# A second queue for the first loads and another bank for the parameters, in the opening of a one-core layer kernel

## The chip, the cores and the metric

One core of one Trainium2 chip. The metric is the device time of one execution in microseconds (us), told as the median of several executions. A profiled execution also leaves a trace, whose span is some 2.2 us shorter than the device time; statements about single waits come from traces, statements about what is faster from the times. In the traces PE is TensorE (matmuls), PEld its weight loads, DVE VectorE, ACT ScalarE, POOL GpSimd, and SPq and ACTq are the queues on which SyncE and ScalarE issue transfers.

## The reference

```python
x  = A_x                                  # (1, 2048, 448), bf16
xn = layernorm(x)                         # over the last axis, 448 wide
s  = state_space(xn, ...)                 # complex recurrence over 2048 steps, plus xn * Dskip
g  = silu((silu(xn @ w_gate) * (xn @ w_up)) @ w_down)    # 448 -> 1792 -> 448
return x + s * g
```

For the change only the very beginning matters: the first 128-row tiles of `x` are normalised and transposed, and multiplied with the first 512 columns of `w_gate` and `w_up`.

## The kernel before

The work is cut into four blocks of 512 rows (four tiles of 128). The opening treats the first block in two halves: tiles 0 and 1 (the left half, banks called `one`) while tiles 2 and 3 are still being normalised, then tiles 2 and 3 (the right half, banks called `gp` and `up`). Warm-up matmuls on constants keep TensorE busy until data is there.

```python
warm(12, D)                       # 12 pairs of 448-column matmuls on constants
load_x1(0)                        # tile 0, SyncE's queue
load_x(1, 3)                      # tiles 1 and 2 in one transfer, SyncE's queue
nc.scalar.activation(of_table[:], half_pi[:], ACT.Sqrt)      # makes ScalarE load its table
load_w(Wg, B_w_gate, 0, 512)
load_x1(3)
for c0, h in ((0, H2), (256, H1)):                           # up weights in two halves of columns
    load_w(Wu, B_w_up, c0, c0 + 256, part=0)
    nc.sync.dma_start(out=Wu[h, KF, 0:512], in_=B_w_up[blk(KF), 0:512][h])
# ... further weights and tiles ...
```

`rb` holds the right half's four banks, two pairs of one for gate and one for up. Before they hold sums they take the transposes of tile 2 (pair 0) and tile 3 (pair 1), and the turned parameters:

```python
def turn_tile(n, half):
    tps = [halves_of(b[:, half[0] : half[1]].bitcast(BF16))[:, 0] for b in rb[n - 2]]
    turned(n, tps)                                           # eight transposes on TensorE
    nc.vector.tensor_copy(out=xT_of(n)[:, :, H1], in_=tps[0])
    ...                                                      # H2: VectorE for tile 2, ScalarE for tile 3

def third():                      # runs between the left half's matmuls
    turn_tile(2, left)

def fourth():                     # likewise, eight matmuls later
    tv = params_turned(rb[0][0][:, right[0] : right[1]])     # two matmuls into pair 0's gate bank
    turn_tile(3, right)
    nc.vector.tensor_copy(out=pcol[:], in_=tv)
    power(dtv[:], euler[:], pcol[:, 0:KT, 0])

def right_half():                 # tile 2 for both pairs, then tile 3 for both pairs
    for f0, c, kw in ((0, left, dict(steps=tiles)), (2, right, dict(late=True))):
        gu_matmuls(0, ...)
```

In the left half the up matmuls come as six that need the first half of the up weights' columns, six that need the second half, tile 2's transposes, eight, the parameters and tile 3's transposes, eight.

## Time and profile before

| before | us |
|---|---|
| device time, median of 3 | 183.27 |
| device time in the rounds with the changed kernel, median of 6 | 183.12 (182.75 to 183.39) |
| span of the profiled execution | 180.9 |

To read the opening, cut it at five events of TensorE: the first transposes, tile 2's transposes, the right half's first matmul and the first full-width (512-column) matmul. This is the table of stretches of the kernel before (columns: stretch, length, then busy time and number of instructions of PE, PEld, DVE, ACT and POOL, granted clock, share of the DMA engines, GB/s).

```profile
0.00:5.59 5.59, 3.79 (x24) 1.74 (x24) 2.91 (x21) 2.56 (x6) 3.73 (x14) 1.00 0.67 192
5.59:8.70 3.11, 3.00 (x78) 2.56 (x80) 2.37 (x10) 2.61 (x7) 0.00 (x0) 1.00 0.93 251
8.70:10.15 1.45, 1.42 (x38) 1.07 (x33) 1.16 (x5) 1.07 (x4) 0.00 (x0) 1.00 1.08 369
10.15:13.30 3.15, 3.15 (x72) 2.81 (x73) 1.72 (x5) 1.33 (x5) 0.45 (x1) 1.00 1.07 358
13.30:180.90 167.60, 164.22 (x1303) 79.51 (x1297) 156.81 (x233) 115.36 (x239) 10.28 (x10) 1.00 0.22 55
```

Only the lengths matter here. The busy column does not show what is lost: a matmul's modelled end lies 0.1 us and more behind the point at which the next can start, so a TensorE that waits 0.2 us still reads as busy. The last stretch, 93% of the span, is the part that no one touches.

### The profile page before, as it was taken

How to read it: one execution, taken by the hardware profiler on the slowest of the kernel's cores; microseconds unless marked ns; L12 is line 12 of the kernel's file. 1: busy time of each engine (PE TensorE's matmuls, PEld its weight loads, DVE VectorE, ACT ScalarE, POOL GpSimd, SP SyncE). 2: the span in 40 equal slices, each digit the busy share in tenths (PEclk: the TensorE clock that was granted, in tenths of full speed). 3: DMA queues.
4: the chain of work that ended last, by engine and by line, in shares of the span. 5: the costliest groups of instructions: out<-in, count | busy, mean ns of one | idle time of the engine just before them, and what ended most of it. 6: DMA issues, size and time to landing. Idle time of an engine off the chain costs nothing.

```text
span 180.9 us, 3868 instructions
## 1 busy us (share of the span) xinstructions
PE 175.6 (97%) x1507; PEld 87.7 (48%) x1507; DVE 165.0 (91%) x271; ACT 122.9 (68%) x258; POOL 14.5 (8%) x24
## 2 busy tenths in 40 slices
PE   8799999999999999999999999999999999999992
PEld 3684444544444555555454444455454444455551
DVE  4869799999999989989999999999999999999962
ACT  4758779997789999298689675943268778601110
POOL 7012400000000000700000001400000000000001
PEclk9999999999999999999999999999999999999999
DMA  5998564899000000035000000052000000001111
GB/s 154 284 363 233 107 121 87 150 252 372 16 0 4 2 0 4 0 71 149 2 4 0 0 4 0 3 113 80 27 0 4 0 0 4 0 0 51 51 62 43
DMA packets 25330, 12.72 MB, mean 70 GB/s; under 512 B 14944, under 2 KB 25312, under 8 KB 25312
## 3 DMA queue, kind: packets, MB, share of 16 engines
q1 hardware_dynamic: 25040, 12.41, 25.7%
q8 instruction: 12, 0.20, 0.4%
q10 hardware_dynamic: 144, 0.07, 0.1%
q14 instruction: 6, 0.05, 0.1%
q0 software_dynamic: 128, 0.00, 0.0%
HBM read 7.23 MB, written 1.84 MB: 50 GB/s over the span
## 4 chain that ended last, share of the span: by engine, by line
PE 95%; DMA 2%; DVE 1%; SPq 0%; issue 0%
PE gp L477 26%; PE hd L620 23%; PE up L477 20%; PE y L658 12%; PE pb L477 12%; PE one L477 2%; DMA x_all<-in_A_x_dram 2%; DVE xn L281 0%; DVE stats_of L269 0%; DVE ob L684 0%; SPq L138 0%; DVE t L680 0%; PE tp L333 0%; PE gp L333 0%; PE y L664 0%
## 5 line engine op out<-in xcount | busy, mean ns | idle before, releaser
L477 PE MATMUL gp<-xT,Wg 64*128 64x512 bf16 (+2 forms) x400 | 82.4, 364 | 0.0
L477 PE MATMUL up<-xT,Wu 64*128 64x512 bf16 (+2 forms) x400 | 82.3, 364 | 0.0
L477 PEld LDWEIGHTS <-Wg 64*128 64x128 bf16 x444 | 38.4, 94 | 24.1
L477 PEld LDWEIGHTS <-Wu 64*128 64x128 bf16 x428 | 38.1, 94 | 19.0 <-issue 0.2
L620 PE MATMUL hd<-Wd,Vt 128*128 128x448 bf16 x224 | 43.5, 352 | 0.0
L607 ACT ACTIVATE gs<-gp 128x512 bf16<-128x512 f32 x52 | 31.4, 605 | 14.0 <-PE gp L477 13.9
L620 PEld LDWEIGHTS <-Vt 128*128 128x128 bf16 x224 | 21.8, 98 | 20.5 <-issue 0.2
L608 ACT ACTIVATE us<-up 128x512 bf16<-128x512 f32 x52 | 31.7, 609 | 0.0
L625 ACT ACTIVATE sg<-hd 128x448 bf16<-128x448 f32 x16 | 8.6, 536 | 25.0 <-PE hd L620 24.3
L477 PE MATMUL pb<-xT,BT 64*128 64x512 bf16 (+1 forms) x224 | 21.9, 349 | 0.0
L612 DVE TENSOR_TENSOR Vt<-gs,us 128x2048 bf16<-128x2048 bf16 (+1 forms) x16 | 17.1, 1075 | 0.3 <-ACT us L608 0.3
L477 PEld LDWEIGHTS <-BT 64*128 64x128 bf16 x224 | 10.7, 94 | 11.4 <-issue 0.7
L551 DVE TENSOR_TENSOR_SCAN bu_re<-rcol,H_re,ere 128x512 bf16<-128x512 f32 x12 | 15.1, 1269 | 0.1
L658 PE MATMUL y<-C,H_re 128*128 128x448 bf16 (+2 forms) x68 | 15.1, 342 | 0.0
L512 ACT ACTIVATE bu_re<-pb 128x512 bf16<-128x512 f32 (+1 forms) x20 | 10.0, 530 | 4.8 <-PE pb L477 4.8
L658 PE MATMUL y<-C,H_im 128*128 128x448 bf16 (+2 forms) x51 | 11.9, 342 | 0.0
L551 DVE TENSOR_TENSOR_SCAN bu_im<-rcol,H_im,eim 128x512 bf16<-128x512 f32 x9 | 11.4, 1263 | 0.0
L317 ACT ACTIVATE xn<-x_all,off_of,rstd 128x384 bf16<-128x384 bf16 (+1 forms) x16 | 8.1, 587 | 3.6 <-POOL off_of L311 3.6
L522 ACT ACTIVATE bu_im<-bu_re 64x512 bf16<-64x512 bf16 x16 | 10.0, 628 | 0.3
L680 DVE TENSOR_TENSOR t<-t,sg 128x448 f32<-128x448 f32 x15 | 9.4, 625 | 0.9
L684 DVE TENSOR_TENSOR sg<-t,x_all 128x448 bf16<-128x448 f32 x15 | 9.4, 625 | 0.5
L545 DVE TENSOR_TENSOR tmp<-bu_im,ST 128x2048 bf16<-128x2048 bf16 x8 | 9.7, 1218 | 0.0
(122 smaller groups left out, 183.8 us busy)
## 6 DMA issues: line engine op xcount, KB each, us to landing
out_dram<-sg SPq DMA_DIRECT2D x15, 112.0 KB, 1.7
Wd<-in_B_w_down_dram SPq DMA_DIRECT2D x1, 1568.0 KB, 10.1
Wg<-in_B_w_gate_dram SPq DMA_DIRECT2D x3, 384.0 KB, 5.1
x_all<-in_A_x_dram SPq DMA_DIRECT2D x1, 896.0 KB, 5.6
Wu<-in_B_w_up_dram SPq DMA_DIRECT2D x4, 192.0 KB, 4.5
Wu<-in_B_w_up_dram SPq DMA_DIRECT2D x2, 384.0 KB, 5.5
x_all<-in_A_x_dram SPq DMA_DIRECT2D x3, 224.0 KB, 5.4
Wg<-in_B_w_gate_dram SPq DMA_DIRECT2D x3, 128.0 KB, 4.9
```

The source lines that it names most:

```text
L477: mm = nc.tensor.matmul(out[:, a:b], lhsT=w[h, d, :], rhs=xT[h, d, q * W + c0 + a : q * W + c0 + b], start=(first and m == 0 and cut is cu ...
L512: nc.scalar.activation(to, pair[i][0], ACT.Copy)
L522: nc.scalar.activation(out[a], in_[b], ACT.Copy)
L545: nc.vector.tensor_tensor(out=of(out, n), in0=of(a, n), in1=of(b, n), op=op)
L551: nc.vector.tensor_tensor_scan(out=T["b"][c][:, k, :], data0=rcol[:, k : k + 1].to_broadcast([P, W]), data1=T["e"][c][:, k, :], initial=in ...
L607: nc.scalar.activation(gs[:, i + j, :], gp_[:], ACT.Silu)
L608: nc.scalar.activation(us[:, i + j, :], up_[:], ACT.Copy)
L612: nc.vector.tensor_tensor(out=Vt[:, f0 : f0 + n, :], in0=gs[:, 0:n, :], in1=us[:, 0:n, :], op=ALU.mult)
L620: nc.tensor.matmul(hd, lhsT=Vt_of[q][:, fi, j * P : (j + 1) * P], rhs=Wd[:, fi, :], start=(fi == 0), stop=(fi == NF - 1),)
L658: nc.tensor.matmul(y[:, c0:c1], lhsT=h, rhs=C2[:, n, c0:c1], start=(n == 0), stop=(n == NS - 1))
L680: nc.vector.tensor_tensor(out=t[:], in0=y, in1=sg[:, c0:c1], op=ALU.mult)
L684: adds.tensor_tensor(out=ob, in0=t[:], in1=x_all[:, m, c0:c1], op=ALU.add)
```

## The change

The intent: tiles 1 and 2 are issued by ScalarE at once instead of by SyncE as its second transfer; the weights behind them move up; the parameters go to tile 3's bank, so that the right half's first pair is free of them, and the right half goes pair by pair, so that tile 3's bank is wanted later; one warm-up pair less makes room for the earlier tiles.

```diff
-    def load_x(n0, n1):
-        nc.sync.dma_start(
+    def load_x(n0, n1, eng=nc.sync):
+        eng.dma_start(
@@
-    warm(12, D)
+    warm(11, D)
     load_x1(0)
-    load_x(1, 3)
+    load_x(1, 3, nc.scalar)
@@ in sums(..., by_tile=True)
+            order = [(n, two, cut) for cut in cuts for n, two in enumerate(pairs)]
+            if not by_tile:
+                order.sort(key=lambda o: o[0])
@@ in fourth()
-        tv = params_turned(rb[0][0][:, right[0] : right[1]])
+        tv = params_turned(rb[1][0][:, left[0] : left[1]])
@@ in right_half()
-        for f0, c, kw in ((0, left, dict(steps=tiles)), (2, right, dict(late=True))):
+        for f0, c, kw in ((0, left, dict(steps=tiles, by_tile=False)), (2, right, dict(late=True))):
```

More of the change, by code (lines that the diff above doesn't have):

```diff
@@ L461, in told_of, with sums @@
         tc.add_manual_dep(mm.ins, notice, SYNC, reason="other half")
-    def sums(q, pairs, eng=nc.gpsimd, turn=False, late=False, behind={}, steps=None):
+    def sums(q, pairs, eng=nc.gpsimd, turn=False, late=False, behind={}, steps=None, by_tile=True):
         left = []
@@ L470, in sums @@
             cuts = steps if steps and first else [None]
-            for n, two, cut in [(n, two, cut) for cut in cuts for n, two in enumerate(pairs)]:
+            order = [(n, two, cut) for cut in cuts for n, two in enumerate(pairs)]
+            if not by_tile:
+                order.sort(key=lambda o: o[0])
+            for n, two, cut in order:
                 for m in range(4 - share):
```

## The prediction

> **What bounds the kernel now.** I read the page first: its busy row and its chain that ended last.
>
> ```profile
> PE 175.6 (97%) x1507; PEld 87.7 (48%) x1507; DVE 165.0 (91%) x271; ACT 122.9 (68%) x258; POOL 14.5 (8%) x24
> PEclk9999999999999999999999999999999999999999
> ...
> PE 95%; DMA 2%; DVE 1%; SPq 0%; issue 0%
> ```
>
> The reader is to see one engine, PE (the TensorE), busy nearly throughout at a full granted clock, and 95% of the chain on it. No line of the matmuls gets shorter by this change, so it can only take away time in which TensorE stands still. Next, therefore, the chain in order of time for the first 16 us (columns: start us, length us, what): everything that is not a matmul lies there, and in the last 4 us, which the change doesn't touch.
>
> ```profile
> 1.18 3.01 DMA x_all<-in_A_x_dram
> 4.19 0.02 issue
> 4.21 0.64 DVE stats_of L269
> ...
> 5.65 0.41 DVE xn L281
> 6.05 0.05 issue
> 6.10 0.29 PE tp L333 x8
> 6.39 0.06 PE warm L191 x2
> 6.45 2.42 PE one L477 x56
> ...
> 9.68 0.44 PE one L477 x8
> 10.12 0.03 issue
> 10.15 0.21 PE gp L477
> ```
>
> The chain begins with the transfer of tiles 1 and 2 (issued at 1.18, landed at 4.19), goes through tile 1's statistics, normalised tile and transposes, and is on TensorE from 6.10. The third view is the timeline, which shows the two places concerned: the start, and the change-over from the left to the right half near 10 us (start, length, engine, line, operation, idle before).
>
> ```profile
> 0.72 1.28 ACT L198 ACT_TABLE_LOAD   x1 [0.72 <-PEq L909]
> 0.72 0.40 SPq L138 DMA_DIRECT2D x_all<-in_A_x_dram  x1
> ...
> 1.18 0.42 SPq L141 DMA_DIRECT2D x_all<-in_A_x_dram  x1
> ...
> 2.85 0.63 DVE L269 BATCH_NORM_STATS2 stats_of<-x_all 128x6 f32<-128x448 bf16 x1 [1.04 <-DMA x_all<-in_A_x_dram]
> ...
> 3.33 0.77 PEld L191 LDWEIGHTS <-const-bfloat16-1.0 64*128 64x128 bf16 x8 [0.20 <-issue]
> ...
> 3.51 0.20 DVE L270 BATCH_NORM_AGGREGATE mv<-stats_of 128x2 f32<-128x9 f32 x1
> ...
> 4.21 0.63 DVE L269 BATCH_NORM_STATS2 stats_of<-x_all 128x6 f32<-128x448 bf16 x1 [0.51 <-DMA x_all<-in_A_x_dram]
> ...
> 9.72 0.29 DVE L745 COPY xT<-gp 128x256 bf16<-128x256 bf16 x1 [0.21 <-PE gp L333]
> 9.75 0.38 ACT L749 ACTIVATE xT<-up 128x256 bf16<-128x256 bf16 x1 [0.36 <-PE gp L333]
> ...
> 9.93 0.17 DVE L757 COPY pcol<-gp 128x20 f32<-128x20 f32 x1
> ...
> 10.15 0.21 PE L477 MATMUL gp<-xT,Wg 64*128 64x128 bf16 x1
> ```
>
> At the start, VectorE is done with tile 0 at 3.71 and stands for 0.51 us until tile 1 lands at 4.19. At the change-over, the last eight matmuls of the left half start at 9.50 and take four steps of about 0.109 us (two run side by side), so the stream could go on at about 9.93. The right half's first matmul starts at 10.15, which is 0.05 us after the end of the pcol copy (9.93 + 0.17 = 10.10). The page's other semaphore steps are as long: xn ended at 6.05 and its transposes began at 6.10. The copy on ScalarE ends at 10.13 and would have let it start at 10.18 only. So this gap of 0.22 us waits for the parameters to be read out of the bank that the right half writes first, though the wait list shows no such wait and the chain books those 0.2 us as matmul time.
>
> **What the Trainium skill says.** "DMA: Bandwidth & Descriptors", section "Issuing engines are not separate DMA queues": transfers issued by different engines share the same 16 DMA engines and interleave; a second issuer saves only issue time. The trace agrees so far as it goes: between 1.75 us and 4.25 us, where the two x loads (115 KB and 229 KB) land, the GB/s row of the first 10 us, in slices of 0.25 us, adds up to some 595 KB, so at least 250 KB of weights moved among them. "TensorE: Matmul & The Clock Gate", section "What's actually happening": half clock until about 3.4 us of activity. Here the step from one warm-up pair to the next is 0.37 us (starts 1.09, 1.46, 1.84) and becomes 0.19 us (eight loads in 0.77 us from 3.33), so the step to full speed came about 2.6 us after the first warm-up matmul at 0.76; the mean clock column stays at 1.00 and hides this. "PSUM — Partial Sum Buffer", section "PSUM bank collisions raise a hardware error": guard by bank, not by address. This is why a copy from one half of a bank holds up a matmul into the other half, and the 10.10 to 10.15 step agrees. "ScalarE: Activation LUTs", section "What ACT_TABLE_LOAD costs": about 1283 ns for the load; the trace has 1.28 us.
>
> **The change part by part.**
>
> 1. *ScalarE issues the load of tiles 1 and 2.* Removed: one SyncE issue of 0.42 us ahead of the weights; they are issued 0.46 us earlier (from 1.65 to about 1.19). Added: an issue of about 0.4 us (the ScalarE issue near the end of the trace takes 0.37) ahead of the table load, which then runs from about 1.18 to 2.46, and the small activation behind it to 2.66. ScalarE's next work is at 3.74, so 1.1 us are left and this costs nothing. Moved: the issue of the load from 1.18 to 0.72, 0.46 us earlier. If all of it arrived, the landing would be 3.73, and VectorE, free at 3.71, would gain 0.48 to 0.50. But tile 0's load, 115 KB, moves at the same time and is in front: at the 230 GB/s of the 2 to 4 us stretch it takes 0.5 us of the engines, in which tiles 1 and 2 must share. What can be won is the share of the engines that stands empty (they are about 70% busy from 1.75 to 2.25, and the rate is at 133, 269, 190, 154 GB/s in the first four slices, against over 360 later), and the weights, also earlier, take their part. I choose a landing at 3.9, a gain of 0.3 us, of 0 to 0.5 possible. From there to the first real matmul all is a chain of fixed steps: statistics begin 4.21, xn ends 6.05, transposes 6.10, so a shift of 0.3 stays 0.3.
> 2. *One warm-up pair less.* The last pairs step at 0.19 us, so the warm-up ends at about 4.36 in place of 4.55 (all at half speed: 0.76 + 11 x 0.37 = 4.83 plus its last matmul's tail). The first transposes start at 5.59 now and would start at 5.3. Off the path: 0 us; it keeps TensorE free if the transposes come earlier.
> 3. *Parameters in tile 3's bank; right half pair by pair.* Now both pairs do tile 2, then both tile 3. The new order does pair 0 with tile 2 (8 matmuls, four steps of 0.055 = 0.22 us), pair 0 with tile 3, then pair 1. Pair 0's banks held only tile 2's transposes, copied out at 9.50. So it starts at 9.93, runs to 10.15, and needs tile 3 from there: VectorE's copy ends at 10.01, ScalarE's at 10.13, plus 0.05 makes 10.18. Pair 1's bank, with the parameters, is free at 10.10 and wanted at 10.40. Instead of 0.22 us of standing, 0.03: a gain of 0.19 us. No instruction is added.
>
> Sum: 0.3 + 0 + 0.19 = 0.49 us, rounded to 0.5. Does it reach the end? Between 20 and 170 us every 10 us window shows TensorE busy 10.00 of 10.00, so nothing there waits for another engine now. VectorE is nearly as full (94% from 20 to 181), but its last wait, 1.58 us before 176.96, is for TensorE: that much it can lag without setting the end. The nearest other limits are the transposed tiles 4 to 7, issued up to 30.4 us and landing 2.4 to 4.0 us after each issue (the last issue begins near 29.2) while the second block's matmuls begin at 33.87, and ScalarE's evictions between 30 and 40 us (9.93 of 10 us busy). Their slack, by these numbers, is 0.6 us or more, and SyncE also comes earlier. So 0.5 us should pass: 183.27 - 0.5 = 182.77, say 182.8.
>
> **The rivals.**
>
> A. *The transfer is hidden in the engines' sharing.* Tile 0 and tiles 1 and 2 split the engines; tile 0 lands later, say 3.1 to 3.3, and tiles 1 and 2 at about 4.1. For it: the skill's sentence, and the 250 KB moved besides. Against it: the low rate in the first slices, and tile 0 is issued no later than now. Then only the 0.19 us of part 3 stay: about 183.1. If tile 0 also came 0.5 late, VectorE would be done with it only at 4.2 and part 1 would give nothing at all.
>
> B. *Everything works and the load lands by 3.7.* VectorE's work on tile 0 then becomes the bound; gain 0.5 + 0.19 = 0.69, about 182.6.
>
> C. *A later engine takes the gain back.* If the transposed tiles or the eviction stage near 33 to 37 us don't move while TensorE comes 0.5 earlier, a new wait of 0.1 to 0.5 us appears there: 182.9 to 183.2. Against it: the slack above.
>
> D. *The shorter warm-up changes the clock.* If in some runs the step to full speed falls after the warm-up, the first blocks run at half speed: their 2.4 us of left-half matmuls would cost up to 2 us more, about 184.5. For it: one pair less in a stretch that barely holds one such window. Against it: the step came 1 us before the warm-up's end, and the gap to the transposes gets shorter, not longer.
>
> **Range and chances.** Of the weights I give, 50% to the sum as chosen (182.6 to 182.95), 25% to A, 10% each to B and C, 5% to D. The three times of before spread over 0.33 us. The range that should hold it 8 times in 10 is 182.35 to 183.25. Two per cent are 3.7 us, over seven times the sum and more than rival D could cost: faster by over 2% 0.005, slower 0.01, within 2% 0.985.
>
> **What would show it.** Right: the issue of tiles 1 and 2 on ScalarE's queue at 0.72; tile 0's statistics still begin at about 2.85 to 2.95; tile 1's at about 3.9; first transposes at about 5.3; the first left-half matmul at about 6.1; in the change-over the gap shrinks from 0.22 to under 0.1 us; all later matmul stages 0.5 us earlier; a span of about 180.4. Wrong: tile 0's statistics start after 3.1 (A); the gap near 10 us stays because a copy other than pcol's ends it; a TensorE wait at 33 us (C); warm-up steps of 0.37 us to the end (D).

## The result, and the profile after

| | before | changed |
|---|---|---|
| median device time, us | 183.12 | 182.40 |
| lowest to highest of 6 | 182.75 to 183.39 | 182.25 to 182.85 |
| span of the profiled execution, us | 180.9 | 180.4 |

The ratio is 0.9965, with a 95% interval of 0.9948 to 0.9981. Ratios here are the mean time of one kernel's fast runs over that of the other's of the same rounds, so not quite the ratio of the medians. It is 0.64 us (0.35 to 0.95) of 183.1: within 2%, clear of noise, and 182.4 lies in the predicted range. A repetition of the changed kernel (e8 below) gave 0.9963.

The same table of stretches for the changed kernel, cut at the same events:

```profile
0.00:5.16 5.16, 4.29 (x22) 1.74 (x22) 2.78 (x21) 2.42 (x6) 3.85 (x14) 1.00 0.67 206
5.16:8.60 3.44, 3.19 (x79) 2.48 (x81) 2.67 (x10) 2.94 (x7) 0.00 (x0) 1.00 0.93 255
8.60:9.71 1.11, 1.11 (x39) 1.06 (x35) 0.69 (x3) 0.51 (x3) 0.00 (x0) 1.00 1.05 329
9.71:12.83 3.12, 3.12 (x76) 3.00 (x73) 1.60 (x6) 1.56 (x6) 0.44 (x1) 1.00 1.05 349
12.83:180.40 167.57, 164.24 (x1303) 83.17 (x1298) 157.01 (x233) 115.36 (x239) 10.46 (x10) 1.00 0.22 56
```

The differences are -0.43, +0.33, -0.34, -0.03 and -0.03 us, together -0.50. So the total of the prediction (-0.49) is met, but not by its terms: the start gives more than the 0.3 predicted and loses most of it in the next stretch, and the change-over gives more than 0.19. The last stretch is the same, so the gain does reach the end.

The timeline of the changed kernel shows where (start, length, engine, line, operation, idle before; the lines of the helper for sums moved from 477 to 480):

```profile
0.72 0.40 SPq L138 DMA_DIRECT2D x_all<-in_A_x_dram  x1
0.73 0.46 ACTq L141 DMA_DIRECT2D x_all<-in_A_x_dram  x1
...
1.22 1.28 ACT L198 ACT_TABLE_LOAD   x1 [1.22 <-PEq L912]
...
3.05 0.63 DVE L269 BATCH_NORM_STATS2 stats_of<-x_all 128x6 f32<-128x448 bf16 x1 [1.24 <-DMA x_all<-in_A_x_dram]
...
3.82 0.58 DVE L269 BATCH_NORM_STATS2 stats_of<-x_all 128x6 f32<-128x448 bf16 x1
...
8.26 0.22 PEld L480 LDWEIGHTS <-Wu 64*128 64x128 bf16 x6 [0.43 <-DMA Wu<-in_B_w_up_dram]
```

Tile 0 now lands later, its statistics starting at 3.05 (2.85 before), and tile 1's statistics follow without a wait at 3.82 (4.21 before). Then comes what was not there before: the load of weights for the second six up matmuls waits 0.43 us for the up weights to land. The chain that ended last now leads through SyncE's issues to this landing (start, length, what), where in the kernel before it led through the transfer of tiles 1 and 2:

```profile
3.12 0.57 SPq L203
3.73 4.49 DMA Wu<-in_B_w_up_dram
8.21 0.05 issue
8.26 0.50 PE one L480 x6
```

The second half of the up weights is issued at 3.73, half a microsecond earlier than before (4.24), and still lands only at 8.21. Its issue in the DMA view (KB, us from issue to landing), first in the kernel before, then in the changed one:

```profile
Wu<-in_B_w_up_dram SPq DMA_DIRECT2D x1, 192.0 KB, 3.9
Wu<-in_B_w_up_dram SPq DMA_DIRECT2D x1, 192.0 KB, 4.5
```

So before it landed at 4.24 + 3.9, about 8.15. TensorE's loads of these weights began there only 0.1 us later:

```profile
8.27 0.21 PEld L477 LDWEIGHTS <-Wu 64*128 64x128 bf16 x4
```

About 0.1 us was thus all that an earlier start could gain at this point, and it could be read before the change was made.

The change-over, first in the kernel before, then in the changed one (timeline, as above):

```profile
8.82 0.60 PE L477 MATMUL one<-xT,Wu 64*128 64x256 bf16 x8
...
9.02 0.29 DVE L745 COPY xT<-gp 128x256 bf16<-128x256 bf16 x1
...
9.36 0.17 PE L350 MATMUL gp<-pick,vseg 64*128 64x20 bf16 x1
...
9.50 0.62 PE L477 MATMUL one<-xT,Wu 64*128 64x256 bf16 x8
```

```profile
8.71 0.60 PE L480 MATMUL one<-xT,Wu 64*128 64x256 bf16 x8
...
9.15 0.17 PE L350 MATMUL gp<-pick,vseg 64*128 64x20 bf16 x1
...
9.27 0.27 PE L480 MATMUL one<-xT,Wu 64*128 64x256 bf16 x1
...
9.71 0.22 PE L480 MATMUL up<-xT,Wu 64*128 64x128 bf16 x1
```

Eight matmuls take four steps of 0.109 us, 0.44 us. In the changed kernel the parameters come 0.44 us after the eight up matmuls before them began, and the right half 0.44 us after the last eight: nothing stands. In the kernel before it was 0.54 us and 0.65 us. The second is the wait that the prediction had found. The first it had overlooked: tile 2's copy ends at 9.02 + 0.29 = 9.31, and the parameter matmuls, into the other half of the same bank, start 0.05 us later, at 9.36.

### The profile page after: what moved, and what is told of

The parts are those of the page before. It is cut to its first block, busy times and chain, and to the rows that moved or that the text cites.

```text
span 180.4 us, 3866 instructions
## 1 busy us (share of the span) xinstructions
PE 175.9 (98%) x1505; PEld 91.5 (51%) x1505; DVE 164.7 (91%) x271; ACT 122.8 (68%) x258; POOL 14.7 (8%) x24
## 4 chain that ended last, share of the span: by engine, by line
PE 94%; DMA 2%; SPq 2%; DVE 0%; issue 0%
PE gp L480 25%; PE hd L623 24%; PE up L480 20%; PE y L661 12%; PE pb L480 12%; DMA Wu<-in_B_w_up_dram 2%; PE one L480 1%; SPq L148 0%; SPq L138 0%; SPq L203 0%; SPq L153 0%; DVE ob L687 0%; DVE t L683 0%; PE y L667 0%; PE gp L333 0%
## 5 line engine op out<-in xcount | busy, mean ns | idle before, releaser
L480 PEld LDWEIGHTS <-BT 64*128 64x128 bf16 x224 | 11.6, 94 | 10.5 <-issue 0.7
```

What stands on the lines that cost most here:

```text
L480: mm = nc.tensor.matmul(out[:, a:b], lhsT=w[h, d, :], rhs=xT[h, d, q * W + c0 + a : q * W + c0 + b], start=(first and m == 0 and cut is cu ...
```

## The experiments

**Theory.** The early load brings TensorE to the up weights before they have landed; they land between 7.7 and 8.3 us whether they are issued at 4.24 or at 3.73, so most of what the load gives is taken back there. The bank gives some 0.34 us, because two waits on that bank go. **Rivals.** That the wait for the up weights was chance of one execution, so that the load gives its 0.43 us as a rule; that only the change-over wait went (0.19 us); that the order of the right half, not the bank, did it; that the warm-up pair is worth its own length. All outputs are right. Within a run the fast device times spread over 0.3 to 0.8 us, in e2 over more, at least as much as the effects.

### e1: the load alone

```diff
 # kernel before
-    load_x(1, 3)
+    load_x(1, 3, nc.scalar)
```

> Kernel before, with the load of tiles 1 and 2 on ScalarE alone (12 warm-up pairs, old bank, old order). Theory (the gain at the start is eaten by a new wait for the up weights): first left-half matmul at about 5.96 instead of 6.39 us, then a stand of 0.3 to 0.45 us before the second six up matmuls near 8.2 us, waiting for the second half of the up weights; right half's first matmul at about 10.04 instead of 10.15, so a gain of about 0.1 us at the end (span 180.8). Rival (the wait for the up weights was chance of one profiled run): no such wait, right half at about 9.72, gain 0.43 us.

Measured: 182.82 us median of 5 against 182.94 before, ratio 0.9996 (0.9982 to 1.0009): no gain that can be told from none. The trace's right half starts at 9.96 (10.15 before, 10.04 expected). The expected stand near 8.2 us is missing, for a reason neither theory had: all twelve warm-up pairs stepped at 0.37 us here, and the warm-up still ran when tile 0's normalised rows were ready (VectorE ended them at 4.99, the transposes began at 5.20), and the matmuls behind it went slowly, so TensorE came to the second six at about 8.2, when the up weights (3.73 + 4.4, about 8.1) had just landed.

```profile
4.45 0.17 PEld L191 LDWEIGHTS <-const-bfloat16-1.0 64*128 64x128 bf16 x2 [0.20 <-issue]
```

This is the twelfth pair's weight load, 0.37 us after the eleventh (4.08); in the first trace of before the last four pairs went at 0.19 us. What follows: in this trace the transposes came 0.39 us earlier than in the kernel before (5.20, 5.59), but the first up matmul only 0.19 (7.86, 8.05), and so did the right half. The 0.20 us between went into slow matmuls right after the warm-up: the first eight transposes take 0.45 us here, 0.29 before. So the load alone is worth little, and here it is the warm-up, not the up weights, that takes half of it.

### e2 and e7: the bank and the order alone

```diff
 # changed kernel
-    warm(11, D)
+    warm(12, D)
-    load_x(1, 3, nc.scalar)
+    load_x(1, 3)
```

> Kernel before, with the parameters in tile 3's bank and the right half pair by pair alone (12 warm-up pairs, load on SyncE). Theory (two bank waits go: the one for the parameter matmuls on tile 2's copy, 0.10 us, and the one at the change-over, 0.21 us): parameter matmuls at about 9.26 instead of 9.36, right half's first matmul at about 9.83 instead of 10.15, gain about 0.31 us. Rival (as predicted before: only the change-over wait goes): right half at about 9.96, gain 0.19 us. In both no wait for the up weights near 8.2 us, since TensorE comes to them as late as in the kernel before.

The profiled execution of e2 fell into the slow state: 268.38 us, a mean granted clock of 0.66. Nothing is read from it. Its other five took 182.34 to 184.76 us; ratio 1.0008, but with an interval of 0.9971 to 1.0044, which settles nothing. The same kernel was run again:

> The kernel with the bank and the order alone once more, because its profile fell into a state with a granted clock of 0.66 and can't be compared. Theory: parameter matmuls right behind the eight up matmuls before them, right half's first matmul 0.4 to 0.45 us after the last eight up matmuls of the left half begin (0.65 before), together 0.3 us less than before from tile 2's transposes to the right half; time 0.2 to 0.35 us below before. Rival (the prediction's 0.19 us, only the change-over): 0.65 to 0.45 there, but the parameters as late as before, time 0.1 to 0.2 us below before.

Measured: 182.67 us median of 6 against 183.15, ratio 0.9975 (0.996 to 0.999), some 0.46 us, more than the 0.2 to 0.35 expected, though these lie within the interval. The timeline of e7 at the change-over:

```profile
8.85 0.60 PE L480 MATMUL one<-xT,Wu 64*128 64x256 bf16 x8
...
9.29 0.17 PE L350 MATMUL gp<-pick,vseg 64*128 64x20 bf16 x1
...
9.41 0.27 PE L480 MATMUL one<-xT,Wu 64*128 64x256 bf16 x1
...
9.85 0.22 PE L480 MATMUL up<-xT,Wu 64*128 64x128 bf16 x1
```

0.44 us and 0.44 us again, and 1.11 us from tile 2's transposes (8.74) to the right half (9.85), as in the changed kernel. Every trace with the old bank has 1.44 or 1.45 there (before, its repetition e11, e1, e6 and e9), and every fast trace with the new one 1.11. So the bank takes 0.34 us off, wherever the rest lies. No wait for the up weights here, as expected of both.

### e3: twelve warm-up pairs in the changed kernel

```diff
 # changed kernel
-    warm(11, D)
+    warm(12, D)
```

> Changed kernel with 12 warm-up pairs again. Theory: where the clock steps up within the warm-up, no difference at all; where all pairs step at 0.37 us, the warm-up ends at about 5.42 instead of 5.05, the first transposes start about 0.26 us later (5.42), but the wait for the up weights near 8.2 us takes that up, so the right half starts within 0.05 us of 9.71 either way and the time within 0.1 us of the changed kernel. Rival (the pair removed is worth its own length at the end): 0.2 to 0.37 us slower than the changed kernel.

Measured: 182.39 us median of 5 (changed kernel: 182.40), ratio to before 0.9973 (0.996 to 0.9986). All twelve pairs stepped at 0.37 us, the transposes started at 5.20 although tile 0 was ready at 5.05, the first left-half matmuls went slowly, and the second six up matmuls then no longer waited; the right half started at 9.77 against 9.71. So the twelfth pair's cost is absorbed where the changed kernel waits for the up weights, and the rival's 0.2 to 0.37 us is not seen. The transposes came 0.2 us earlier than expected: twelve pairs hold TensorE to 5.20, not 5.42.

### e4: the right half tile by tile, parameters in tile 3's bank

```diff
 # changed kernel
-        for f0, c, kw in ((0, left, dict(steps=tiles, by_tile=False)), (2, right, dict(late=True))):
+        for f0, c, kw in ((0, left, dict(steps=tiles)), (2, right, dict(late=True))):
```

> Changed kernel with the right half tile by tile again (parameters still in tile 3's bank). Theory (the bank is what matters, the order little): the right half starts at 9.71 as in the changed kernel, then stands after its first 8 matmuls at about 9.93 until the last copy out of tile 3's bank, about 0.05 us: loss 0.05 us or less against the changed kernel. Rival (the order is what opens the gap): first stop of 0.2 us, loss 0.2 us.

Measured: 182.52 us median of 4, ratio to before 0.9973 (0.9956 to 0.999). In the trace, tile 2's transposes at 8.49 and the right half at 9.60, 1.11 us as in the changed kernel; from there to the first full-width matmul (12.79) 3.19 us against 3.12. So the bank opens the gap and the order saves 0.07 us of a new one, a little more than expected and far from the rival's 0.2.

### e5 and e12: the up weights whole

```diff
 # changed kernel
-    for c0, h in ((0, H2), (256, H1)):
-        load_w(Wu, B_w_up, c0, c0 + 256, part=0)
-        nc.sync.dma_start(out=Wu[h, KF, 0:512], in_=B_w_up[blk(KF), 0:512][h])
+    load_w(Wu, B_w_up, 0, 512)
```

> Changed kernel with the first 512 columns of the up weights in one pair of transfers with 1024-byte rows (384 KB and 128 KB) instead of two halves with 512-byte rows and two half-height pieces. Theory (the new wait is for bytes that come slowly, at 150 to 270 GB/s from 5.5 to 7.25 us, because the rows are short): the rate stays above 300 GB/s there, the up weights land before 7.6 us, the wait of 0.43 us near 8.2 us is gone, right half's first matmul at about 9.4 instead of 9.71, about 0.3 us faster than the changed kernel. Rival (the rate is low there for another reason): the first up matmuls wait, even longer since the whole has to land, and it is 0.3 us or more slower.

Measured: the rate holds, and the wait shrinks to 0.16 us, now at the first up matmuls (weight load at 7.43), to which TensorE came earlier than in any other trace. The row of GB/s over the first 10 us in slices of 0.25 us, first of the changed kernel, then of e5:

```profile
GB/s 0 0 0 0 0 0 0 100 111 212 362 380 355 373 348 377 377 356 339 349 342 328 266 148 164 232 203 168 193 303 313 326 299 320 340 332 315 328 328 316
```

```profile
GB/s 0 0 0 0 0 0 0 204 337 369 367 243 224 250 287 315 353 356 337 307 316 277 309 349 328 310 275 312 332 340 352 377 389 381 381 385 392 378 371 360
```

From 5.5 to 7.25 us (slices 23 to 29) the changed kernel moves 148 to 266 GB/s and e5 275 to 349. The right half started at 9.21. But the median of 6 was 182.43 us, ratio to before 0.9966, no better than the changed kernel: the 0.3 us expected in time did not come.

> The changed kernel with whole up weights once more, since its first trace was 0.5 us shorter at the right half than the changed kernel's but its median time was the same. Theory (with the up weights in time, the start of tile 0's statistics alone sets the beginning, and it varies): the right half's first matmul comes 6.4 to 6.6 us after tile 0's statistics start, no wait for the up weights; with a start of 2.75 to 3.05 us that is 9.2 to 9.6 us, time 182.2 to 182.5. Rival (another wait appears in most runs): the wait list of TensorE's loads shows the weights again, or the distance is over 6.7 us; time 182.4 to 182.9.

Measured: no wait for the up weights, and the right half 6.34 us after tile 0's statistics (6.44 in e5, with its wait), slightly under the range given. But these statistics started at 3.23 us, later than in any trace of the changed kernel (3.05, 2.89), so the right half came at 9.57. Time 182.43 us, ratio 0.9963 (0.9947 to 0.9978). So with whole up weights the new wait is 0.16 us in one trace and gone in the other, and tile 0's landing, which varies by half a microsecond, becomes the limit; a gain in time over the changed kernel is not shown.

### e6: the up weights whole, in the kernel before

```diff
 # kernel before: the same edit as in e5
```

> Kernel before with the up weights whole as in the run beside it. Theory (before, nothing waited for the up weights): no change in where TensorE stands until 10.15 us, time within 0.1 us of before. Rival (before was held up by them too, unseen): 0.2 us or more faster.

Measured: 183.33 us median of 6 against 183.11, ratio 1.0011 (0.9994 to 1.0028): no gain, and the 0.2 us of loss are not clear of noise. As the theory held, with the old loads the up weights cost little in time (that they can be waited for, e11 shows). The two traces can't be compared at the start, since tile 1 happened to land late in e6, with its statistics at 4.64 instead of 4.21.

### e8: the changed kernel again

```diff
 # no edit
```

> The changed kernel once more, for a second trace. Theory: tile 0's statistics at 2.75 to 3.05 us, tile 1's follow without a wait; the second six up matmuls wait again for the up weights, 0.2 to 0.5 us, ending at 8.1 to 8.3 us, if TensorE gets to them before 8 us. Rival (the wait was chance): up weights landed before 7.7 us, no wait, right half at about 9.4 us. Time within 0.15% of its first runs (182.1 to 182.7).

Measured: 182.55 us median of 6 against 183.15, ratio 0.9963 (0.9946 to 0.9979). Tile 0's statistics at 2.89, tile 1's behind them at 3.66, and the wait is there again, longer, since TensorE arrived earlier, and it ends at the same time:

```profile
8.26 0.22 PEld L480 LDWEIGHTS <-Wu 64*128 64x128 bf16 x6 [0.59 <-DMA Wu<-in_B_w_up_dram]
```

The wait is a bit over the 0.2 to 0.5 us expected. e4's trace has it too (0.46 us, ending at 8.14). So it is no chance of one trace: of the four traces with the changed loads, eleven warm-up pairs and the up weights in two halves, three have it (the changed kernel, e4, e8) and one has not (e9, next).

### e9: the load with eleven warm-up pairs

```diff
 # kernel before
-    warm(12, D)
+    warm(11, D)
-    load_x(1, 3)
+    load_x(1, 3, nc.scalar)
```

> Kernel before with the load on ScalarE and 11 warm-up pairs (old bank, old order). Theory (what the earlier load gives is taken back, by the warm-up where it is long and by the up weights where it isn't): transposes at about 5.1, a stand for the up weights near 8.2, right half at about 9.95 to 10.05, time 0.1 to 0.2 us below before, as with 12 pairs. Rival (the twelfth pair was all that kept the load's gain back): right half at 9.7 or before, time 0.4 us below before.

Measured: 182.98 us median of 6 against 183.15, ratio 0.9986 (0.9972 to 1.0000), about 0.26 us, between the theory's 0.1 to 0.2 and the rival's 0.4, with an interval from none to 0.5: the time doesn't decide. Its trace is the rival's picture: the up weights had landed at 7.7 us (3.72 + 4.0), no stand, the right half at 9.69. That execution took 182.55 us; the other five took 182.88 to 183.10. So the up weights are sometimes in time, and then the load is worth what it gives at the start; the slower five were not traced.

### e10: two loads on ScalarE and whole up weights

```diff
 # e5
-    load_x(1, 3, nc.scalar)
+    load_x(1, 2, nc.scalar)
+    load_x(2, 3, nc.scalar)
```

> Changed kernel with whole up weights, and tile 1 and tile 2 as two loads of 115 KB, both issued by ScalarE, a try at a version that beats both. Theory (tile 0 lands late because 229 KB on the other queue share its engines): with 115 KB beside it tile 0 lands about 0.1 us earlier, statistics of tile 0 at about 2.75, of tile 1 right behind; no wait for the up weights; right half at 9.2 or before; 0.3 us faster than the changed kernel in the trace and 0.1 to 0.4 in time. Rival (tile 0's landing doesn't depend on what runs beside it): as the whole up weights alone, 182.4.

Measured: 182.89 us median of 6 (182.78 to 183.44) against 183.15, ratio 0.999: this try at a better version failed. Tile 0's statistics started at 3.28, later rather than earlier. So less beside tile 0 in that first transfer did not bring it sooner, and what exactly delays it is open. The trace shows a second cost, of the split itself: tile 2 landed only at about 4.7, ScalarE waited 0.31 us for it and so came to tile 1's root at 5.26 (4.86 in e12), and the right half began 6.56 us after tile 0's statistics instead of 6.34.

### e11: the kernel before again

```diff
 # no edit
```

> The kernel before once more, for a second trace of its start. Theory: tile 0's statistics at 2.6 to 2.9 us, tile 1's only at 4.1 to 4.7, since its load is issued second on the same queue; under 260 GB/s on average from 2 to 4 us; the right half's first matmul follows 0.65 us after the last eight up matmuls begin, the parameters 0.05 us after the first copy of tile 2 ends. Rival (the late landing in the first trace was chance): tile 1's statistics at 3.8 or before.

Measured: 183.09 us in one execution. Tile 0's statistics at 2.78, tile 1's at 3.80, earlier than the theory's range (4.1 to 4.7) and just at the rival's bound: the landing of the second load on SyncE's queue varies by up to 0.8 us (3.80, 3.90 in e7, 4.21, 4.64). With the tiles early, the kernel before meets the same barrier:

```profile
6.33 1.37 PEld L477 LDWEIGHTS <-Wg 64*128 64x128 bf16 x38 [0.18 <-DMA Wg<-in_B_w_gate_dram]
8.31 0.22 PEld L477 LDWEIGHTS <-Wu 64*128 64x128 bf16 x6 [0.22 <-DMA Wu<-in_B_w_up_dram]
```

Its transposes began at 5.18, 0.41 us earlier than in the first trace, yet its right half at 10.10, 0.05 us earlier: the 0.4 us are lost to the gate and up weights. This is the cleanest showing of the theory, since the kernel is the same and tile 1 came 0.4 us earlier by chance. The first gate weights came later in return, at about 5.9 against 5.4 (1.65 plus 4.2 and 3.7).

## Why the prediction was right or wrong

**The total was right.** Predicted 182.8 us, measured 182.40, in the range; predicted a shift of 0.49 us in the trace, found 0.45 (last matmuls 177.27 to 176.82) to 0.50 (span). That it fits so well is luck in part: the load was taken 0.20 us too high and the bank 0.15 too low, and the two nearly cancel.

**Part 1, the load: right in its mechanism, wrong in what it is worth.** "I choose a landing at 3.9, a gain of 0.3 us" became a landing at about 3.6 (0.73 + 2.9), statistics at 3.82 and transposes 0.43 us earlier, more than the term. Tile 0 lands later, as rival A held (3.05), but not late enough to matter: VectorE went from tile 0 straight to tile 1, which is the bound named in rival B. What failed is the step that let this gain pass down the line: the fixed chain ("a shift of 0.3 stays 0.3") ends at the first real matmul, near 6.4 us, the check that the gain reaches the end begins at 20 us, and of the weights between it was said only that they are "also earlier". They are issued 0.5 us earlier and land no earlier: by issue and time to landing at 7.7 to 8.3 us in the three traces with the old loads and halved up weights (before, e7, e11), at 7.7 to 8.2 in the six with the new (changed, e1, e3, e4, e8, e9). TensorE had 0.1 us to spare there. The stretch from the transposes to tile 2 grew by 0.33 us, so part 1 left 0.10. Rival C had this form (a later wait takes the gain back), but looked for it near 33 us.

**Part 2, the warm-up: right in its size.** It is worth nothing in time here (e3). Its reckoning at 4.36 held for one clock phase only; in this trace all eleven pairs stepped at 0.37 us to the end, the sign given for rival D, and the transposes still waited for their data, because 11 slow pairs end in time. A cost of rival D's kind, some matmuls at half speed after the warm-up, shows with twelve pairs: from the first transposes to the first up matmul it is 2.46 us before and in the changed kernel, 2.66 in e1, 2.81 in e3 and 2.80 in e7; with eleven pairs the first eight transposes are slow in e10 (0.40 us against 0.29). (D's sum is a little off: 182.8 plus up to 2 us is up to 184.8, not 184.5.)

**Part 3, the bank: right mechanism, too small a term.** "Instead of 0.22 us of standing, 0.03: a gain of 0.19 us" measured 0.34 us to the right half's first matmul, in every pair of traces. The change-over alone gave 0.21; 0.10 came from the parameter matmuls' own wait on tile 2's copy, in plain sight in the timeline at 9.31 to 9.36, which the prediction didn't look for; the rest, 0.03, lies among the transposes of tiles 2 and 3. The order saves 0.07 against e4, 0.03 of it against the kernel before.

**The sum by the runs**: 0.10 + 0.34 + 0.03 + 0.03 = 0.50 us in the trace. In time, the bank and order alone gave 0.46 us and the load with eleven pairs 0.26, together 0.72 against 0.64 to 0.68 for both, within their intervals. Open: what sets the up weights' landing. It isn't the bytes moved alone: by 8.0 us the transfer engines had moved about 1760 KB in the changed kernel and 1630 before (the GB/s rows of 0.25 us added up), and the weights landed no earlier. e5 changes both the length of rows and the half-height pieces. Open too: why the warm-up's slow pace lasts longer in some traces, and what makes tile 0's landing vary from 2.77 to 3.28 us with the second queue.

## What to carry to other kernels

When a first transfer is moved forward, follow the engine that profits to the next data it needs, and ask when that lands: an earlier issue on transfer engines that other transfers share need not land earlier. Look also for how long that data lies ready before it is used: 0.1 us here. A wait that the wait list doesn't show can be found by arithmetic: matmuls that should step by a fixed time and don't, and a copy out of the same bank that ends 0.05 us before they go on; having found one, look for all readers of that bank. Effects of 0.3 us in the first 10 us of a kernel vary by as much from execution to execution, so take several traces before believing one.

## What the Trainium skill lacked or had wrong

- "DMA: Bandwidth & Descriptors", section "Issuing engines are not separate DMA queues": a second issuer saves only issue time. At the start of a kernel this saving counts, and it has a price the section doesn't give. From 2 to 4 us the nine fast traces with ScalarE as second issuer moved 291 to 328 GB/s, the four without it 217 to 253; tile 0's statistics, in turn, began at 2.77 to 3.28 us instead of 2.65 to 2.85. The runs don't separate the earlier issue from the second queue.
- The same page, section "Specifications", gives 512 bytes as the smallest transfer for full rate. Here the rate fell to 148 to 266 GB/s while 512-byte rows and half-height pieces came, and stayed at 275 to 349 with 1024-byte rows (changed kernel and e5, 5.5 to 7.25 us). The runs don't separate the rows from the pieces, so the figure is not shown to be wrong.
- "TensorE: Matmul & The Clock Gate", section "What's actually happening", puts the step to full speed at about 3.4 us of activity, varying by 500 ns. It came 2.6 us after the first warm-up matmul in the first trace of before, while in e1, e3, e6 and e7 all twelve pairs still stepped at 0.37 us, the last starting 4.1 us after the first: a spread of over 1 us.
- The same page, section "Seeing it yourself", names a clock of 13/16 with three or more busy cores of a die. With one core in use, one execution (e2) ran at a mean granted clock of 0.66, steady at 0.65 from 6 us on, and took 268.38 us; no page consulted has this.
- "PSUM — Partial Sum Buffer", section "PSUM bank collisions raise a hardware error": nothing wrong, but no cost is given. Sharing one bank between a copy and matmuls into its other half cost 0.34 us here in two waits, 0.05 us of each being the step from the copy's end to the next matmul.
